# An attention kernel with a feed-forward behind it: the value products change bank and tile, the first feed-forward product its order, and the weight decoding its pace

## The chip, the cores and the metric

The kernel runs on one core of a Trainium2 chip. The metric is the time of one execution in microseconds on the device; the time before is the median of three runs. The core has TensorE (PE, matrix products, writing into the eight banks of PSUM), VectorE (DVE), ScalarE (ACT), GpSimd (POOL) and SyncE (SP), whose queue issues nearly all DMA transfers. Each engine takes its instructions in order and waits for others by semaphores.

## What is computed

Attention over 8 batches of 8 heads with 576 positions and 64 features, with a threshold below each row's maximum, and then a feed-forward layer over the 4608 tokens of 512 features:

```python
scores = scale * np.matmul(q, k.transpose(0, 1, 3, 2))
thresh = np.max(scores, axis=-1, keepdims=True) - tau
scores = np.where(scores >= thresh, scores, -1000000000.0)
attn = np.exp(scores - np.max(scores, axis=-1, keepdims=True))
attn = attn / (np.sum(attn, axis=-1, keepdims=True) + 1e-09)
attn_out = np.matmul(attn, v)
# x: the heads side by side, (4608, 512)
h = x @ w_in                       # (512, 2048)
sp = np.where(h > 20.0, h, np.log1p(np.exp(np.minimum(h, 20.0))))
return (h * np.tanh(sp)) @ w_out   # (2048, 512)
```

The weights arrive as 64-bit floats, and the kernel makes 32-bit numbers of them itself ("decoding"): one bit pattern from the upper word by a scale, a clamp, a shift and a sign, one from the lower word, and their sum; then an upper part that TensorE reads at its fast 32-bit format (hi) and a remainder (lo). Products are made from such pairs of parts.

## The kernel before

**Tiles.** Two heads make a pair; 32 pairs of 9 tiles of 128 query rows are 288 tiles, numbered g, with t = g % 9 the place in the pair. One iteration of the main loop issues the steps of several tiles, each a few tiles behind the one before: the scores of tile g+1 (`begin`; tile `s`, two buffers of two PSUM banks), the maximum, the exponential and the mask of tile g (`row_max`, `exponential`, `masked`; tiles `st`, `e`, `p`), the normalisation of g-1 on POOL, the transposes of g-2 (`transposes`; bank `tp`, and for odd tiles and t = 8 also the last keys, bank `t5`, which the profile names `t`), and the copies of g-3 out of PSUM on ACT (`evacuate`; tiles `hi`, `lo` for even and odd tiles from `tp`, `tk` from `t5`). `tp` and `t5` have one buffer each. All engines but SP are wrapped so that they keep the order in which the program issues (line 95 is that wrapper, which is why all rows of the profile carry it).

**Product with the values.** A pair's nine tiles are gathered in two groups (0 to 3 and 4 to 8). The product `y` of a group (`values_full`) is closed at t = 3 and t = 8 by `CLOSE`, `lag` = 4 tiles later, so at t = 7 and t = 3. It is cut in five chunks, which `pieces` hands out: two in an iteration before tile `SOON` = 38, five from there on. `gather` copies y on ACT into `x`; from `SOON` on in the same iteration as the last chunk, before that in the next. `y` takes one of the two buffers `ph` in the pool `psh`, which the first feed-forward product `h` takes too. When a pair is closed, `split_x` makes the parts `xh` (ACT) and `xl` (POOL) of its two token halves, two tiles apart.

**First feed-forward product.** `gemm1(b)` runs one batch behind the attention, from tile 36b + 42 on. It is a generator of 384 matmuls; `EVEN[g % 9]` says how many of them an iteration issues, none where `y` is made. For each token half c and each of the 16 feature blocks f it sums 12 matmuls into a bank `h`, which ACT copies to `hst`, and SP stores. Batches 0 to 6 take c outermost; the last one takes the feature halves outermost.

**Weights of the first product.** 32 pieces of 128 x 256 are decoded during the first tiles. `W1_STEPS` lists at which of each 18 tiles a piece is started (12 of 18). After its load, a piece goes through stages in successive iterations: two empty ones, the scaling on ACT, `clamp` (POOL), then `shift` and `sign` (DVE) and `add` (POOL), an empty one, `upper` (ACT) and `lower` (POOL, or DVE for the nine pieces of `ONV`). The sign is issued ahead of the mask of its tile before tile `JOIN` = 39, and behind it from there on.

**Queues.** SP issues the loads of q, k, v and weights and the stores of hst; a load waits there until its buffer is free, and what stands behind it in the queue waits too. Splits of q and k follow their loads two tiles later (`LOADS`).

After the attention the last batch's first product and the second product run (`w2`, `z`, `g`, `o`); the change does not touch them.

Of the kernel before, what the change touches and what calls it, by code (L numbers as in the profile page):

```python
# [15 lines left out]
B, H, S, D = 8, 8, 576, 64  # L16
NP = H // 2
LOADS = ((1, 0, 1, 3, 2, 3, 7, 3, 5, 8), (0, 3, 3, 2, 5, 4, 5, 8, 8, 9), (0, 0, 2, 4, 5, 4, 7, 6, 7, 8), (0, 0, 1, 3, 2, 3, 7, 5, 7, 8))
W1_STEPS = (1, 3, 4, 6, 7, 8, 10, 12, 13, 15, 16, 17)
STAGES = ((0, 1, 1), (0, 1, 1))  # L20
THIRD = ((),)
LAG = 2
# [7 lines left out]
SOON = 9 * FULL + 2  # L30
ONP = 1
ONV = (3, 9, 11, 12, 14, 15, 17, 18, 22)
JOIN = 39
PLAIN = (0, 1)
DM, DF = 512, 2048
ND, NF = DM // P, DF // P
# [33 lines left out]
LAST = {1: 0, 4: 1, 6: 2, 8: 3}  # L70
TURN = [[(t % 2, t // 2 * P + t % 2 * P)] for t in range(8)] + [QCOL[4]]
CLOSE = {3: 0, 8: 1}
EVEN = (14, 14, 14, 0, 13, 14, 14, 0, 13)
WIDTH = (256, 320, 320, 256)
XOFF = (0, 256, 256, 0)
SCALE = 1.0 / float(D) ** 0.5
# [42 lines left out]
class Decode:  # L119
# [16 lines left out]
        nc.scalar.activation(c, low, AF.Copy, scale=2.0**-29)  # L136

    def clamp(self):
        self.nc.gpsimd.tensor_scalar(fv(self.b), fv(self.a), TOP_MAX, -TOP_MAX, ALU.min, ALU.max)

    def shift(self):
        self.nc.vector.tensor_scalar(self.a, self.b, 3, 0x7FFFFFF8, ALU.logical_shift_left, ALU.bitwise_and)
# [18 lines left out]
def attention_moe(tc, q, k, v, tau, w_in, w_out, out):  # L161
# [3 lines left out]
    with ExitStack() as outer:  # L165
# [105 lines left out]
        with ExitStack() as first:  # L271
# [6 lines left out]
            with ExitStack() as att:  # L278
# [160 lines left out]
                def transposes(g):  # L439

                    both = tiles[g]["both"]
                    at = odd(g) * (S + D)
                    tp = pst.tile([P, 4, P], F32, name="tp")
                    for c in range(4):
                        nc.tensor.transpose(tp[:, c, :], both[:, at + c * P:at + (c + 1) * P], ident)
                    t5 = None
                    last = g < 9 * VP and g % 9 == 8
                    if odd(g) or last:
                        t5 = pst.tile([P, P], F32, name="t5")
                        if last:  # L450
                            nc.tensor.transpose(t5, both[:, S - P:S], ident)
                            nc.tensor.transpose(t5[:D], both[:, S - D:S], ident)
                        else:
                            nc.tensor.transpose(t5, both[:, 4 * P:5 * P], ident)
                    return tp, t5

                def evacuate(t, tp, t5, pt):
                    r = t // 4 if t < 8 else 1
                    if r not in pt:
                        pt[r] = [  # L460
                            ptp.tile([P, w, 320], F32, name=n, tag=n) for n, w in (("hi", 4), ("lo", 4), ("tk", 1))
                        ]
                    tail = pt[r][2][:, 0]
                    if t < 8:
                        a, at = t % 2, t // 2 % 2 * P
                        nc.scalar.copy(pt[r][a][:, :, at:at + P], tp)
                        if a:
                            nc.scalar.copy(tail[:, at:at + P], t5)
                        return
                    for a in range(2):  # L470
                        rows = slice(a * D, (a + 1) * D)
                        nc.scalar.copy(pt[r][a][:, :, 2 * P:], tp[:, :, rows])
                        nc.scalar.copy(tail[rows, 2 * P:], t5[rows, rows])
# [30 lines left out]
                    for hi, lo, t5 in tails(g):  # L504
                        nc.vector.tensor_tensor(lo, t5, fv(hi), ALU.subtract)

                def values_full(r, pt, vf, x):
                    main, tail = pt[r][:2], pt.pop(r)[2]
                    n = (2 + r) * P - r * D
                    y = psh.tile([P, 512], F32, name="y", tag="ph")  # L510

                    def chunk(c):
                        for a in range(2):
                            rows = slice(a * D, (a + 1) * D)
                            m = main[a][:, c, :n] if c < 4 else tail[:, 0, :n]
                            nc.tensor.matmul(y[rows, :n], vf[:, a, c], m, start=c == 0, stop=c == 4)

                    def gather():
                        nc.scalar.copy(x[:, r * QT:r * QT + n], y[:, :n])

                    return [lambda c=c: chunk(c) for c in range(5)], gather
# [21 lines left out]

                    return gather

                def split_x(g, x):
                    parts = []
                    for c in range(2):
                        xh = xpool.tile([P, HB], F32R, name="xh", bufs=12)
                        xl = xpool.tile([P, HB], F32R, name="xl", bufs=12)  # L550
                        parts.append((xh, xl))

                    def half(c):
                        xh, xl = parts[c]
                        sl = slice(c * HB, (c + 1) * HB)
                        nc.scalar.copy(xh, x[:, sl])
                        nc.gpsimd.tensor_tensor(xl, x[:, sl], fv(xh), ALU.subtract)

                    chores.setdefault(g + XSPLIT[1], []).append(lambda: half(0))
                    chores.setdefault(g + XSPLIT[1] + XSPLIT[2], []).append(lambda: half(1))  # L560
                    return parts
# [14 lines left out]
                def gemm1(b, xs, bank=shared, first=1):  # L576

                    halves = (range(NF // 2), range(NF // 2, NF))
                    if b < B - 1:
                        order = [(c, f) for c in range(2) for fs in halves for f in fs]
                    else:
                        order = [(c, f) for fs in halves for c in range(2) for f in fs]
                    banks = {}
                    made = {}

                    def parts(c, f, ds):
                        if (c, f) not in banks:  # L590
                            banks[c, f] = bank("h")
                        h = banks[c, f]
                        half, at = divmod(f * P, DF // 2)
                        for d in ds:
                            xh, xl = xs[d][c]
                            wh, wl = (w[:, d, at:at + P] for w in w1[half])
                            for i, (a, m) in enumerate(((wh, xh), (wh, xl), (wl, xh))):
                                nc.tensor.matmul(
                                    h[:, :HB], a, m, start=d == 0 and i == 0, stop=d == ND - 1 and i == 2
                                )  # L600
                                yield

                    def leave(c, f):
                        if f % 4 == 0:
                            made["hst"] = hp.tile([P, 4, HB], F32, name="hst", tag="hst")
                        hst, h = made["hst"], banks.pop((c, f))
                        if b < B - 1 or f % 2:
                            nc.scalar.copy(hst[:, f % 4], h[:, :HB])
                        else:
                            nc.vector.tensor_copy(hst[:, f % 4], h[:, :HB])  # L610
                        if f % 4 == 3:
                            store(nc.sync, hst, (2 * b + c) * HB, f - 3)

                    for c, f in order[:first]:
                        yield from parts(c, f, range(ND - 1))
                    for n, (c, f) in enumerate(order):
                        steps = parts(c, f, range(ND - 1, ND) if n < first else range(ND))
                        for i in range(3 if n < first else 3 * ND):
                            next(steps)
                            if i == (2 if n < first else 3 * ND - 1):  # L620
                                leave(c, f)
                            yield
# [27 lines left out]
                    made = pairs[pi]["ops"]  # L650
                    tiles[g] = dict(s=scores(t, 0 if odd(g) else D, **made))

                def product(g):
                    pi, t = divmod(g, 9)
                    pr = pairs[pi]
                    if t == (3 if pi < VP else 1):
                        pr["x"] = sm.tile([P, S], F32, name="x", bufs=2)
                    if pi < VP:
                        if t in CLOSE:
                            some, gather = values_full(CLOSE[t], pr["pt"], pr["ops"]["vf"], pr["x"])  # L660
                            pieces.extend((work, None) for work in some[:-1])
                            pieces.append((some[-1], (gather, pi if t == 8 else None)))
                    elif t in LAST:
# [1 line left out]

                def close_pair(g, pi):
                    b, hp = divmod(pi, NP)
                    batches.setdefault(b, []).append(split_x(g, pairs.pop(pi)["x"]))

                warm = psh.tile([P, P], F32, name="warm", tag="ph")  # L670

# [11 lines left out]
                    split()  # L683
                nc.vector.tensor_scalar(back, back, 1.0 / SCALE, None, ALU.mult)
                begin(0)
                for g in range(NT + 5):
                    now = [work.pop(0) for work in decoding]
                    decoding = [work for work in decoding if work]
                    if g + 1 < NT:
                        begin(g + 1)  # L690
                    ahead = 2 <= g < SOON
                    lag = 4 if g < VP * 9 + 4 or VP == NPAIRS else 5
                    if lag <= g < NT + lag and (g != VP * 9 + 4 or VP == NPAIRS):
                        product(g - lag)
                    if 3 <= g < NT + 3:
                        old = ((g - 3) % 9, *tiles[g - 3]["tp"], pairs[(g - 3) // 9]["pt"])
                        full = g - 3 < VP * 9
# [9 lines left out]
                    for _ in range(5 if g >= SOON else PIECES):  # L707
                        if pieces:
                            work, then = pieces.pop(0)
                            work()  # L710
                            if then:
                                (done if g >= SOON else ready).append(then)
                    if g < NT:
                        tiles[g]["st"], tiles[g]["e"] = row_max(tiles[g]["s"])
                    if 1 <= g <= NT:
# [257 lines left out]
```

## Time and profile before

| | |
|---|---|
| median of 3 runs | 1357.99 us (1357.27 to 1361.05) |
| the profiled execution | 1360.66 us, span 1358.9 us |
| PE busy | 1311.3 us (96%) |
| DVE, ACT, POOL busy | 872.4 (64%), 849.5 (63%), 742.3 us (55%) |
| mean granted PE clock | 0.987 |
| attention | scores of tile 0 reduced at 6.7 us, of tile 287 at 917.7 us |

Busy times are those of one execution. Rows in order of time give the start in us, the duration in us, engine, line, operation, tiles (out<-in), shapes and count, and in brackets the idle time of that engine before it and what ended it. Rows of groups give count, then busy us and mean ns of one, then idle us before them. Rows of waits give us in total, times and the longest.

### The profile page before, as it was taken

The numbers are of one execution on the slowest core, as the hardware profiler recorded it, in microseconds if no ns is written. First come the engines' busy times: TensorE is split into PE (matmuls) and PEld (weight loads), VectorE is DVE, ScalarE is ACT, GpSimd is POOL, SyncE is SP. The second block draws the span as 40 slices with busy tenths as digits, with TensorE's granted clock in tenths as the row PEclk, the third lists the DMA queues.
The fourth block names the chain that finished last, engine by engine and source line by source line (L and its number), as shares of the span: only waits on it lengthen the run. The fifth ranks groups of instructions, "written<-read, shape, count | busy, mean of one in ns | idle before, by whom it ended". The sixth has DMA issues, their size and how long they took to land. (4 is left out here: it accounts for less than half of the span.)

```text
span 1358.9 us, 28431 instructions
## 1 busy us (share of the span) xinstructions
PE 1311.3 (96%) x9941; PEld 1171.1 (86%) x9941; DVE 872.4 (64%) x2372; ACT 849.5 (63%) x1676; POOL 742.3 (55%) x1093
## 2 busy tenths in 40 slices
PE   8887999999999999999999999999999999999998
PEld 5444789988889889898888898898979999999998
DVE  6897756555556556566566556564996666666664
ACT  4777766666666666666666666665665555555552
POOL 4899966656556566566565665642403334444431
PEclk9888999999999999999999999999999999999999
DMA  6333443433333333333333333312744343444440
GB/s 175 103 92 115 150 147 89 115 95 99 107 89 97 109 103 93 98 91 114 99 94 106 89 104 102 94 53 84 253 149 155 125 137 113 141 140 137 137 131 32
DMA packets 151904, 154.83 MB, mean 114 GB/s; under 512 B 35536, under 2 KB 128720, under 8 KB 151760
## 3 DMA queue, kind: packets, MB, share of 16 engines
q1 hardware_dynamic: 151760, 153.00, 37.5%
q8 instruction: 79, 1.29, 0.4%
q14 instruction: 65, 0.53, 0.1%
HBM read 105.78 MB, written 47.19 MB: 113 GB/s over the span
## 5 line engine op out<-in xcount | busy, mean ns | idle before, releaser
L95 DVE SCALAR_TENSOR_TENSOR p<-s,st,e 128x576 f32<-128x576 f32 x288 | 235.4, 817 | 331.4 <-ACT e L95 331.0
L95 PE MATMUL h<-xh,w1h 128*128 128x288 f32 x1024 | 302.6, 295 | 1.1 <-ACT hst L95 1.1
L95 PE MATMUL h<-xl,w1h 128*128 128x288 f32 x1024 | 302.4, 295 | 0.0
L95 PE MATMUL h<-xh,w1l 128*128 128x288 f32 x1024 | 302.3, 295 | 0.0
L95 POOL TENSOR_SCALAR p<-p,st 128x576 f32<-128x576 f32 x288 | 240.3, 835 | 108.3 <-DVE st L95 89.2
L95 PE MATMUL s<-k,q 128*128 128x288 f32 (+1 forms) x1280 | 244.3, 337 | 32.4 <-DVE p L95 31.3
L95 POOL TENSOR_TENSOR z<-z 128x256 f32<-128x256 f32 x128 | 124.2, 975 | 223.1 <-DVE z L95 214.3
L95 ACT ACTIVATE e<-s,st 128x576 f32<-128x576 f32 x288 | 215.9, 750 | 45.7 <-DVE st L95 43.0
L95 PEld LDWEIGHTS s<-k,q 128*128 128x128 f32 (+1 forms) x1280 | 172.0, 192 | 55.6 <-DVE p L95 48.9
L95 DVE TENSOR_REDUCE st<-s 128x1 f32<-128x576 f32 x288 | 216.8, 753 | 2.7 <-PE s L95 2.7
L95 DVE TENSOR_TENSOR gl<-z,gh 128x1792 fp32r<-128x1792 f32 (+1 forms) x72 | 141.6, 1967 | 108.2 <-ACT gh L95 108.2
L95 ACT CAST gh<-z 128x1792 fp32r<-128x1792 f32 (+1 forms) x72 | 116.5, 1620 | 150.0 <-issue 81.2
L95 PEld LDWEIGHTS h<-xh,w1h 128*128 128x128 f32 x1024 | 192.6, 188 | 2.0 <-ACT hst L95 1.3
L95 PEld LDWEIGHTS h<-xh,w1l 128*128 128x128 f32 x1024 | 192.5, 188 | 0.0
L95 PEld LDWEIGHTS h<-xl,w1h 128*128 128x128 f32 x1024 | 192.5, 188 | 0.0
L95 PE MATMUL tp<-ident,p 128*128 128x128 f32 x1152 | 180.0, 279 | 3.9 <-POOL p L95 1.5
L95 PEld LDWEIGHTS tp<-ident,p 128*128 128x128 f32 x1152 | 135.9, 141 | 44.3 <-issue 28.6
L95 POOL TENSOR_TENSOR k<-r,k 128x320 fp32r<-128x320 f32 x112 | 97.9, 874 | 95.8 <-ACT k L95 93.6
L95 PE MATMUL y<-hi,vf 128*64 128x320 f32 (+1 forms) x512 | 145.2, 426 | 1.0 <-ACT hst L95 1.0
L95 PE MATMUL y<-lo,vf 128*64 128x320 f32 (+1 forms) x512 | 145.2, 426 | 0.0
L95 PE MATMUL o<-gh,sl 128*128 128x256 f32 x512 | 144.5, 282 | 0.0
L95 PE MATMUL o<-gl,sh 128*128 128x256 f32 x512 | 143.8, 281 | 0.0
(68 smaller groups left out, 2712.0 us busy)
## 6 DMA issues: line engine op xcount, KB each, us to landing
z<-hd SPq DMA_DIRECT2D x144, 256.0 KB, 3.1
r<-q SPq DMA_DIRECT2D x112, 160.0 KB, 2.2
r<-k SPq DMA_DIRECT2D x112, 160.0 KB, 2.4
vf<-v SPq DMA_DIRECT2D x64, 160.0 KB, 2.3
out_t<-c SPq DMA_DIRECT2D x36, 256.0 KB, 2.4
dec<-w_in SPq DMA_DIRECT2D x32, 256.0 KB, 3.2
hd<-hst SPq DMA_DIRECT2D x16, 512.0 KB, 3.3
w<-w_out SPq DMA_DIRECT2D x16, 512.0 KB, 4.5
```

Of the source, the lines that this page charges most:

```text
L95: made = method(*args, **kwargs)
```

## The change

It has five parts.

1. **Bank.** From tile `SOON` + 3 on, `y` is placed in the bank of `t5`, which grows to a whole bank for that (`own`); `psh` is left to `h`. `evacuate` copies `t5` ahead of `tp`.
2. **Tile.** The lag of the product is 5 instead of 4 from tile `SOON` + 2 on, so `y` is made at t = 8 and t = 4; `EVEN` moves its zeros there. The copy of `y` comes an iteration after its last chunk until the last tile (`NT`), not only before `SOON`. The loop has one more iteration.
3. **First batch's first product.** Batch 0 takes the feature halves outermost, and the second token half of its `xh` and `xl` lies in four more buffers of the pool `sm`.
4. **Pace.** `W1_STEPS` starts 10 pieces in 18 tiles instead of 12, so the last of the 32 is started at tile 57 instead of 48. `JOIN` = 72 puts the sign of every piece ahead of the mask.
5. **Clamp.** `clamp` goes from POOL to DVE.

```diff
-W1_STEPS = (1, 3, 4, 6, 7, 8, 10, 12, 13, 15, 16, 17)
+W1_STEPS = (1, 3, 5, 6, 8, 10, 12, 14, 15, 17)
...
-JOIN = 39
+JOIN = 72
...
-EVEN = (14, 14, 14, 0, 13, 14, 14, 0, 13)
+EVEN = (14, 14, 14, 13, 0, 14, 14, 13, 0)
...
     def clamp(self):
-        self.nc.gpsimd.tensor_scalar(fv(self.b), fv(self.a), TOP_MAX, -TOP_MAX, ALU.min, ALU.max)
+        self.nc.vector.tensor_scalar(fv(self.b), fv(self.a), TOP_MAX, -TOP_MAX, ALU.min, ALU.max)
...
-                        t5 = pst.tile([P, P], F32, name="t5")
+                        t5 = pst.tile([P, 512], F32, name="t5")[:, :P]
...
-                        nc.scalar.copy(pt[r][a][:, :, at:at + P], tp)
                         if a:
                             nc.scalar.copy(tail[:, at:at + P], t5)
+                        nc.scalar.copy(pt[r][a][:, :, at:at + P], tp)
...
-                def values_full(r, pt, vf, x):
+                def values_full(r, pt, vf, x, own):
...
-                    y = psh.tile([P, 512], F32, name="y", tag="ph")
+                    home, tag = (pst, "t5") if own else (psh, "ph")
+                    y = home.tile([P, 512], F32, name="y", tag=tag)
...
-                def split_x(g, x):
+                def split_x(g, x, early):
...
-                        xh = xpool.tile([P, HB], F32R, name="xh", bufs=12)
-                        xl = xpool.tile([P, HB], F32R, name="xl", bufs=12)
+                        home, n = (sm, 4) if early and c else (xpool, 12)
+                        xh = home.tile([P, HB], F32R, name="xh", bufs=n)
+                        xl = home.tile([P, HB], F32R, name="xl", bufs=n)
...
-                    if b < B - 1:
+                    if 0 < b < B - 1:
                         order = [(c, f) for c in range(2) for fs in halves for f in fs]
...
-                for g in range(NT + 5):
+                for g in range(NT + 6):
...
-                    lag = 4 if g < VP * 9 + 4 or VP == NPAIRS else 5
-                    if lag <= g < NT + lag and (g != VP * 9 + 4 or VP == NPAIRS):
-                        product(g - lag)
+                    lag = 4 if g < SOON + 2 else 5
+                    if lag <= g < NT + lag and g != SOON + 2:
+                        product(g - lag, g > SOON + 2)
...
-                                (done if g >= SOON else ready).append(then)
+                                (done if g >= NT else ready).append(then)
```

More of the change, by code (lines that the diff above doesn't have):

```diff
@@ L651, in begin, with product @@
                     tiles[g] = dict(s=scores(t, 0 if odd(g) else D, **made))
-                def product(g):
+                def product(g, own):
                     pi, t = divmod(g, 9)
@@ L659, in product @@
                         if t in CLOSE:
-                            some, gather = values_full(CLOSE[t], pr["pt"], pr["ops"]["vf"], pr["x"])
+                            some, gather = values_full(CLOSE[t], pr["pt"], pr["ops"]["vf"], pr["x"], own)
                             pieces.extend((work, None) for work in some[:-1])
@@ L667, in close_pair @@
                     b, hp = divmod(pi, NP)
-                    batches.setdefault(b, []).append(split_x(g, pairs.pop(pi)["x"]))
+                    batches.setdefault(b, []).append(split_x(g, pairs.pop(pi)["x"], b == 0))
                 warm = psh.tile([P, P], F32, name="warm", tag="ph")
```

## The prediction

> **What bounds the kernel now.** I read the page first, then the busy times by stage, then the waits of PE (TensorE) by stage, and last the order of time around the waits that were left. Tile n of the attention begins, in this text, where the VectorE (DVE) maximum of its scores starts.
>
> ```profile
> span 1358.9 us, 28431 instructions
> ```
> The next rows are busy times in stretches: its ends, its length, then us (and number) of PE, PE's weight loads, DVE, ACT (ScalarE) and POOL (GpSimd), and the granted clock.
> ```profile
> 110.10:132.00 21.90, 14.62 (x77) 9.21 (x77) 16.13 (x54) 14.90 (x39) 19.32 (x32) 0.83 0.31 91
> 132.00:205.40 73.40, 70.23 (x510) 60.93 (x510) 50.38 (x167) 50.65 (x126) 58.50 (x92) 0.96 0.47 145
> 205.40:917.70 712.30, 704.05 (x5419) 629.37 (x5419) 420.05 (x1569) 473.45 (x1113) 432.92 (x690) 1.00 0.34 97
> ```
> PE is full but for the beginning: from 205.4 us on it lacks 8.25 of 712.3 us. Up to tile 42, at 132 us, the first product does not exist yet; DVE and POOL are the busy ones, and just before it the granted clock is 0.83. Between 132 and 205.4 PE lacks 3.2 us, and a clock of 0.96 takes up to another 2.9. So the change can win in three places only: the time until tile 42, the 6.1 us behind it, and the 8.25 us of the long stage. The next fence has PE's largest wait in each of the stretches 6.7 to 132, 132 to 205.4 and 205.4 to 917.7 us, and one of the rest of the run (us, times, longest).
>
> ```profile
> PE s L95 <- DVE p L95: 20.2, 22, 2.1
> ...
> PE s L95 <- DVE p L95: 2.9, 4, 2.0
> ...
> PE s L95 <- DVE p L95: 8.2, 24, 0.4
> ...
> PE y L95 <- ACT hst L95: 1.0, 1, 1.0
> ```
> The 24 waits of the long stage come once in each pair of heads (9 tiles), always behind the product with the values, y. In order of time at one of them:
> ```profile
> 332.83 0.43 ACT L95 COPY x<-y 128x320 f32<-128x320 f32 x1 [2.11 <-PE y L95]
> ...
> 334.84 0.76 ACT L95 ACTIVATE e<-s,st 128x576 f32<-128x576 f32 x1
> ...
> 335.64 0.82 DVE L95 SCALAR_TENSOR_TENSOR p<-s,st,e 128x576 f32<-128x576 f32 x1 [3.01 <-ACT e L95]
> ...
> 336.52 0.80 PE L95 MATMUL s<-k,q 128*128 128x288 f32 x4 [0.35 <-DVE p L95]
> ```
> ACT stands 2.11 us at the copy of y, because the copy is issued in the tile that also issues y's matmuls. The exponential e behind it is late, DVE waits 3.01 us for e, the score bank comes free late, and PE stands 0.35 us.
>
> **The change, term by term.** The sum is made against the profiled execution: 1360.7 us, span 1358.9; the median of the runs is 1358.0, 2.7 lower, so I carry the difference over to the median.
>
> *A. Up to tile 42.* The smallest period of a tile, seen where no weight is decoded, is 2.55 us; DVE then has 0.68 us free, waiting for e:
> ```profile
> 20.07 0.82 DVE L95 SCALAR_TENSOR_TENSOR p<-s,st,e 128x576 f32<-128x576 f32 x1 [0.68 <-ACT e L95]
> ...
> 20.82 0.75 DVE L95 TENSOR_REDUCE st<-s 128x1 f32<-128x576 f32 x1
> ...
> 23.37 0.75 DVE L95 TENSOR_REDUCE st<-s 128x1 f32<-128x576 f32 x1
> ...
> 131.97 0.75 DVE L95 TENSOR_REDUCE st<-s 128x1 f32<-128x576 f32 x1
> ```
> Tile 5 starts at 20.82 and tile 42 at 131.97: 37 tiles in 111.15 us, where 37 x 2.55 would be 94.4. The excess is 16.8 us. What it is made of:
> ```profile
> L95 DVE SCALAR_TENSOR_TENSOR dec<-dec 128x256 uint32<-128x256 uint32 x24 | 13.2, 551 | 0.7
> ...
> L95 DVE TENSOR_SCALAR dec<-dec 128x256 uint32<-128x256 uint32 x24 | 12.1, 505 | 2.3 <-POOL dec L95 2.3
> ...
> L95 POOL TENSOR_SCALAR dec<-dec 128x256 f32<-128x256 f32 x24 | 9.5, 398 | 0.0
> ```
> ```profile
> L95 DVE TENSOR_SCALAR dec<-dec x32: 271/320/2421, 24.4 to 172.2; 128x256 uint32<-128x256 uint32 x32
> L95 DVE SCALAR_TENSOR_TENSOR dec<-dec x32: 411/426/1046, 24.7 to 176.3; 128x256 uint32<-128x256 uint32 x32
> ```
> The first fence has decode rows of 16.5 to 132 us, the second the same two of the whole run (min/median/max ns). The shift and the sign of a weight piece take 0.27 and 0.41 us undisturbed, together just the 0.68 that is free. They took 12.1 and 13.2 us for 24 pieces: 24 x 0.27 + 24 x 0.41 = 16.3, so 9.0 us are stretching while POOL works. Another 2.3 us DVE waited for POOL's clamp. The copy of y at tile 40 costs the rest that can be named:
> ```profile
> 124.28 0.16 DVE L95 RECIPROCAL st<-st 128x1 f32<-128x1 f32 x1
> ...
> 125.60 0.42 ACT L95 COPY x<-y 128x320 f32<-128x320 f32 x1 [4.39 <-PE y L95]
> ...
> 126.00 0.78 PE L95 MATMUL s<-k,q 128*128 128x288 f32 x4
> ...
> 127.61 0.76 ACT L95 ACTIVATE e<-s,st 128x576 f32<-128x576 f32 x1
> ...
> 129.48 0.75 DVE L95 TENSOR_REDUCE st<-s 128x1 f32<-128x576 f32 x1
> ```
> With the copy a tile later, e of tile 40 could start near 124.4 instead of 127.61. The next scores are done at 126.8 and become the late thing, so the reduction of 129.48 comes about 2.7 us earlier. After the change 20 pieces instead of 24 are shifted before tile 42 (10 instead of 12 in 18 tiles, five tiles behind their issue); 20 x 0.375 (9.0 / 24) = 7.5 us of stretching. POOL loses a clamp of 0.398 us in two of three tiles, a tenth of its time, so I take 6.8. DVE gains the clamp, which the trace has only on POOL; its nearest row is the shift, the same size and engine: 0.27 undisturbed, 0.505 as a mean, 2.42 at worst. A clamp falls in the tile before its own shift, into the free 0.68; in two tiles of 18 it meets another piece's shift: four such tiles before 42, 4 x 0.5 = 2 us. The wait for POOL's clamp goes. Of the 16.8 us, 9.0 + 2.3 + 2.7 = 14.0 become 8.8: **-5.2 us**. Ends: -14 if all of it goes; +5 if all 20 clamps are exposed at 0.505 against the 5.2.
>
> *B. 132 to 205 us.* The 2.0 us wait of the table above comes from one shift that lasted through three POOL operations:
> ```profile
> 164.95 0.82 POOL L95 TENSOR_TENSOR xl<-x,xh 128x288 fp32r<-128x288 f32 x1
> ...
> 165.03 2.42 DVE L95 TENSOR_SCALAR dec<-dec 128x256 uint32<-128x256 uint32 x1 [0.88 <-POOL dec L95]
> ...
> 165.73 0.87 POOL L95 TENSOR_TENSOR k<-r,k 128x320 fp32r<-128x320 f32 x1
> ...
> 166.55 0.73 POOL L95 TENSOR_TENSOR w1l<-dec,w1h 128x256 fp32r<-128x256 f32 x1
> ```
> The clamps are off POOL, the signs come ahead of the mask, and PE-bound tiles leave DVE slack; but decoding now goes on to tile 65. I take **-3.5** of the 6.1; ends -6.1 and +3 (12 clamps at the shift's 0.505, half of them exposed). The new order of the first product costs nothing: weights of its second half are wanted from tile 60 on (8 feature blocks in 9 tiles, twice), the last piece, issued at tile 57, is done by about 65, and the block that reads it starts near 67; with the old order it would have been wanted at 58. Four more tiles of SBUF hold the second token half; they add no instruction.
>
> *The queues.* The loads of values on SP wait for y, so they come a tile later, with the query loads queued behind them; these are read six tiles or more later, so nothing. Fewer weight loads per tile ease SP.
>
> *C. The long stage.* y's copy is now issued a tile after y, so ACT doesn't stand: **-8.2** if all 24 waits go. Late next can be y itself, 50 times, which now needs the copy of the last keys, tk, out of the same bank:
> ```profile
> 339.44 0.27 PE L95 MATMUL t<-ident,p 128*128 128x128 f32 x1
> ...
> 339.47 0.78 PE L95 MATMUL s<-k,q 128*128 128x288 f32 x4
> ...
> 340.09 0.29 PE L95 MATMUL h<-xh,w1h 128*128 128x288 f32 x1
> ...
> 340.12 0.27 ACT L95 COPY tk<-t 128x128 f32<-128x128 f32 x1
> ...
> 340.22 0.29 PE L95 MATMUL h<-xl,w1h 128*128 128x288 f32 x1
> ```
> t ends at 339.71; PE passes the scores and is ready at 340.09. With tk ahead of lo (the copy of tp, 0.59), ACT can copy from 339.75 to 340.02: PE waits for nothing to 0.1 us, if ACT is free. It need not be:
> ```profile
> 346.30 0.46 ACT L95 CAST k<-r 128x320 fp32r<-128x320 f32 x1
> 346.35 0.27 PE L95 MATMUL t<-ident,p 128*128 128x128 f32 x1
> ...
> 346.66 0.59 ACT L95 COPY lo<-tp 128x512 f32<-128x512 f32 x1
> ```
> Here ACT came free 0.1 us after t. I take 0.06 us x 50 = **+3**; ends 0 and +13 (a whole tk copy, 0.27, each time). In the other direction, t's next transposes need the bank back from the copy of y: ACT has lo (0.59), e (0.76) and the copy (0.43) to do, 1.8 us, while PE does scores and 14 h matmuls at 0.13 us spacing, 2.4 us; hidden. The splits of a batch's last pair move from tile 4 ahead of its product to tile 1 ahead: xl is ready about 4.2 us after the tile starts (lo 0.59, e, y copy, two 0.46 splits, then 0.87 and 0.81 on POOL), wanted after 4.8; six batches, **+0.5**, ends 0 and +3.
>
> *D. The end of attention.* y no longer waits for an h bank: -1.0 us. But the DVE work that ends the run waits for the last x split, which now comes after all of batch 6's matmuls:
> ```profile
> 935.58 0.43 ACT L95 COPY x<-y 128x320 f32<-128x320 f32 x1 [3.01 <-PE y L95]
> ...
> 939.61 0.69 DVE L95 TENSOR_SCALAR s<-w 128x1024 f32<-128x1024 f32 x1 [17.32 <-POOL xl L95]
> ```
> Today it starts 4.1 us behind y, 2.0 of them under 15 h matmuls; afterwards about 2.6 behind y with none: +0.5. Together **-0.5**, ends -1.5 and +1.
>
> Sum: -5.2 - 3.5 - 8.2 + 3 + 0.5 - 0.5 = -13.9; 1358.0 - 13.9 = **1344 us**.
>
> **The rivals.**
> *The port (R1).* DVE's clamps are stretched like the 2.42 us shift, and A and B give nothing: -8.2 + 3 = -5.2 with the rest, 1353. For it: POOL is 88% busy from 110 to 132 us. Against: most clamps fall in tiles without a shift.
> The Trainium skill, "SBUF — State Buffer", section "Who interferes with whom", speaks for R1: a DVE operation in a two-port mode and a GpSimd operation exclude each other for a whole instruction, whichever issues first. The trace agrees that the shift is held up, but 2.42 us through three POOL operations is more than one instruction's turn. By that rule at its hardest, each of 20 clamps behind one POOL operation of 0.87, A would pay 20 x (0.27 + 0.87) less 16 x 0.68 of free time, 11.9 in place of 2, and the time would be 1354.
> *A new wait in the long stage (R2).* y waits for tk or for its own bank about as long as PE stood before, so C is nil: -9, 1349. For it: ACT is 0.1 us late in the row above.
> *Everything goes (R3).* No half clock behind tile 42, the stretching gone: -14 - 6.1 - 8.2 - 1.5 = -30 at the most; half-way from the forecast, -22, 1336.
> *Slower (R4).* ACT is so late that y waits 0.6 us each time (lo and more ahead of tk): 50 x 0.6 = 30, against 16.9 won: +13, 1371. It turns at 0.34 us for each y. Against: the splits leave the tile before.
>
> **How the numbers follow.** Forecast 0.42, R1 0.17, R2 0.17, R3 0.17, R4 0.07. A measurement of this kernel tells about 0.3%, 4 us, from no change. The forecast's own range is 1339 to 1350. With R1, R2 and most of R3 it becomes 1334 to 1355, leaving out R4 and the far end of R3. Faster by over 0.3% (below 1353.9): forecast, R2, R3 and half of R1, 0.84; within: 0.10; slower: 0.06.
>
> **What would show it.** PE's waits for DVE's p in the long stage fall from 24 of 0.35 us to few; ACT's waits for y almost vanish; tile 42 starts near 127; no DVE wait for POOL's clamp. Waits of y for ACT's tk of over 0.1 us, or of h for POOL's xl each 36 tiles, would make C wrong; a mean DVE clamp over 0.7 us would make A and B wrong.

## The result

The changed kernel takes 1336.4 us (median of 4 runs, 1336.1 to 1336.8) against 1357.6 for the kernel before in the same comparison: ratio 0.984, 95% interval 0.9822 to 0.9858. That is 21.2 us faster; 13.9 were forecast. The time lies outside the forecast's own range (1339 to 1350 us) and inside the wider one that takes in the rivals (1334 to 1355); it is the time that the rival R3 had named (1336). The profiled execution took 1336.1 us with a span of 1334.3; its span is 24.6 us shorter than that of before, and not 21.2, mostly because the profiled execution of before (1360.7) lay 3.0 us above the median of this comparison.

The page of the kernel after, and its busy times by stretches: to tile 36, to 42, to 66 and to 287 (ends, length, PE, PE's weight loads, DVE, ACT, POOL, granted clock):

```profile
span 1334.3 us, 28422 instructions
...
PE 1297.9 (97%) x9941; PEld 1167.4 (87%) x9941; DVE 882.6 (66%) x2404; ACT 844.0 (63%) x1676; POOL 735.8 (55%) x1061
```
```profile
6.60:106.70 100.10, 82.12 (x514) 45.67 (x512) 89.46 (x305) 70.53 (x165) 70.01 (x109) 0.95 0.40 121
106.70:128.00 21.30, 14.57 (x77) 9.14 (x77) 17.89 (x56) 15.54 (x40) 17.32 (x26) 0.83 0.40 117
128.00:204.00 76.00, 75.85 (x579) 68.87 (x580) 63.49 (x205) 60.40 (x153) 67.48 (x100) 0.98 0.48 145
204.00:892.50 688.50, 688.50 (x5349) 620.06 (x5348) 414.52 (x1548) 461.62 (x1095) 428.69 (x681) 1.00 0.35 101
```
From tile 66 on PE lacks nothing at all: 688.50 of 688.50 us. From tile 42 to 66 it lacks 0.15 us of 76.0. What is left to win before the end of the attention lies ahead of tile 42, but for the granted clock of 0.98 between 42 and 66.

The same times of every kernel of this study, worked out from the starts of the score reductions. The last column is the mean length of nine tiles, one pair of heads, in the long stage: (start of tile 270 - start of tile 90) / 20. All are us.

| kernel | tile 42 at | 42 to 66 | 66 to 287 | behind 287 | a pair |
|---|---|---|---|---|---|
| before | 132.0 | 82.3 | 703.5 | 441.1 | 28.69 |
| after | 128.0 | 76.0 | 688.5 | 441.8 | 28.07 |
| e1 copy later | 129.8 | 80.5 | 715.6 | 441.8 | 29.15 |
| e2 y moved only | 132.4 | 79.4 | 688.7 | 442.1 | 28.07 |
| e3 y not moved | 129.5 | 79.1 | 703.4 | 441.2 | 28.69 |
| e4 clamp on POOL | 132.0 | 76.9 | 688.5 | 441.8 | 28.07 |
| e5 clamp only | 131.1 | 77.4 | 703.5 | 441.2 | 28.69 |
| e6 pace only | 130.5 | 80.1 | 703.3 | 441.1 | 28.68 |
| e7 tp first | 127.8 | 77.6 | 702.0 | 442.2 | 28.62 |
| e8 same tile | 128.7 | 75.9 | 688.7 | 441.6 | 28.07 |
| e9 splits moved | 131.4 | 78.3 | 689.2 | 441.2 | 28.09 |
| e10 lag only | 130.6 | 79.2 | 688.7 | 441.5 | 28.07 |
| e11 warm | 126.6 | 74.7 | 688.5 | 441.8 | 28.07 |
| e12 without bank | 125.9 | 77.0 | 689.2 | 441.1 | 28.09 |

Each row is one execution. The first two columns are uncertain: e10 and the kernel before are the same program up to tile 42, and they reach tile 36 at 108.3 and 110.1 us and tile 42 at 130.6 and 132.0. From tile 0 to 36 the granted clock was 0.95 in e10 and 0.90 before. Tile 0 itself starts at 6.3 to 7.7 us in the kernels of the table. So differences of up to about 1.8 us in the first column say nothing, and the second, in which the clock varies too, is to be read with the same care. The long stage repeats to 0.2 us.

Of the 24.6 us of the spans, 15.0 were won between tiles 66 and 287, 6.3 between 42 and 66, 4.0 ahead of 42 (2.6 if e10 stands for the kernel before); 0.7 were lost behind 287.

### The profile page after: what moved, and what is told of

The parts are those of the page before. It is cut to its first block, busy times and chain, and to the rows that moved or that the text cites. A ratio compares the mean times of both kernels' runs of the same rounds, so it can differ in the third digit from the quotient of the medians.

```text
span 1334.3 us, 28422 instructions
## 1 busy us (share of the span) xinstructions
PE 1297.9 (97%) x9941; PEld 1167.4 (87%) x9941; DVE 882.6 (66%) x2404; ACT 844.0 (63%) x1676; POOL 735.8 (55%) x1061
## 5 line engine op out<-in xcount | busy, mean ns | idle before, releaser
L95 PE MATMUL s<-k,q 128*128 128x288 f32 (+1 forms) x1280 | 241.1, 333 | 21.1 <-DVE p L95 20.0
L95 ACT ACTIVATE e<-s,st 128x576 f32<-128x576 f32 x288 | 216.1, 750 | 26.9 <-DVE st L95 23.8
L95 ACT COPY hi<-tp 128x512 f32<-128x512 f32 (+1 forms) x160 | 87.0, 544 | 169.4 <-PE tp L95 169.1
L95 PE MATMUL o<-gh,sh 128*128 128x256 f32 x512 | 143.5, 280 | 0.0
```

Source lines behind the costliest of these rows:

```text
L95: made = method(*args, **kwargs)
```

## The long stage: what the stall was, and what took it away

The stall was larger than the row that the prediction used. Waits of the long stage before the change, by PE's weight loads, which run ahead of the matmuls, and by the matmuls:

```profile
PEld s L95 <- DVE p L95: 13.9, 24, 0.6
...
PE s L95 <- DVE p L95: 8.2, 24, 0.4
PEld y L95 <- issue: 8.2, 50, 0.2
```
In order of time, at the wait that the prediction shows:
```profile
335.57 0.60 PE L95 MATMUL tp<-ident,p 128*128 128x128 f32 x4
...
336.52 0.56 PEld L95 LDWEIGHTS s<-k,q 128*128 128x128 f32 x4 [0.59 <-DVE p L95]
```
From the first start of the transposes to the start of the scores it took 0.95 us, where the others of the same shape take 0.36: 0.59 us, the number of the weight loads. The matmul's row counts only from the modelled end of the matmul before it. 24 x 0.59 = 14.2 of the 15.0 us.

After the change, in the long stage:
```profile
ACT hi L95 <- PE tp L95: 155.5, 123, 2.6
...
ACT tk L95 <- PE t L95: 37.6, 73, 1.3
...
PEld y L95 <- ACT tk L95: 8.0, 49, 0.2
```
The wait for DVE's p is gone from PE. ACT now waits for the transposes instead of y. The only wait of y is that of its weight loads for tk, 8.0 us in 49; before, the same loads stood 8.2 us in 50 with nothing to wait for, and where y follows one tile's scores it starts 0.70 us behind their start both before and after. So y's new wait costs nothing. The forecast had +3 us for it.

### Four runs that sort the parts of the move

**e2**: the changed kernel with pace, order, sign and clamp as before (parts 3 to 5 undone).

> The changed kernel with the pace, the order of the first batch's product, the place of the sign and the clamp as before; only bank, lag and copy of y are changed. Theory T: 0.62 us per pair x 27 = -17, tile 40 about -1: 1339 to 1342 us. Rival (the parts need each other, the clamp and the pace made room on VectorE and GpSimd for the long stage): no more than -8: above 1349 us.

Measured: 1343.2 us, ratio 0.9875 (0.9856 to 0.9895), a little above the range expected; a pair 28.07. The whole gain of the long stage is in parts 1 and 2, without help from the decoding.

**e1**: the kernel before and one line.
```diff
-                                (done if g >= SOON else ready).append(then)
+                                (done if g >= NT else ready).append(then)
```


> The kernel before, with one edit: ScalarE's copy of y is issued a tile after y's matmuls in the long stage too; y keeps its bank among the two of h and its lag of 4. Theory T (what counted is that ScalarE no longer stands at y's copy, but that needs a bank of y's own): the stall of 0.6 us per pair of heads goes, and y keeps one of h's two banks a tile longer. From the counts of matmuls, h wants that bank 0.6 + 3 x 0.13 = 1.0 us into the tile behind the longer y, and the copy frees it after about 1.9: a wait of 0.9 us per pair. Net +0.3 us x 25: 1357 to 1366 us. Rival (the later copy is all of it, the bank does nothing): -0.6 x 25 = -15: 1342 to 1345 us.

Measured: 1369.5 us, ratio 1.0077 (1.006 to 1.0094): slower, a pair 29.15. The wait came where the counts had put it:
```profile
PEld h L95 <- ACT x L95: 23.0, 23, 1.0
...
PE h L95 <- ACT x L95: 17.6, 23, 0.8
```
The stall of 0.6 went, and one of 1.0 us for h's bank came, once in a pair; the net 0.46 us a pair is more than the 0.3 expected, and the time lies above the range. So at this place a later copy does need a bank of its own. That is not yet the proof that the later copy was needed.

**e8**: the changed kernel with that one line put back.
```diff
-                                (done if g >= NT else ready).append(then)
+                                (done if g >= SOON else ready).append(then)
```


> The changed kernel with y's copy issued in the tile of y's last chunk again; own bank and lag 5 stay. Theory T (ScalarE standing at that copy makes the stall): the period of a pair returns from 28.07 to about 28.7 us, 15 us in all, ratio to before 0.993 to 0.996. Rival (the bank of its own and the shifted tile do the most): 0.982 to 0.988.

Measured: 1336.6 us, ratio 0.9843 (0.9827 to 0.9859): nothing is lost that could be told, and the long stage takes 688.7 us as against 688.5. ACT stands at y's copy as it did before the change, and PE does not care:
```profile
ACT x L95 <- PE y L95: 81.7, 47, 2.0
```
Here my theory fell, the one of the prediction too: that ACT stands at the copy was not what stopped PE. Left over were the bank and the tile. What else the tile decides is what stands behind the copy in ACT's queue. At t = 3 of the kernel before:
```profile
333.15 0.46 ACT L95 CAST q<-r 128x320 fp32r<-128x320 f32 x1
...
333.52 0.46 ACT L95 CAST k<-r 128x320 fp32r<-128x320 f32 x1
...
333.88 0.43 ACT L95 CAST xh<-x 128x288 fp32r<-128x288 f32 x1
...
334.21 0.58 ACT L95 COPY lo<-tp 128x512 f32<-128x512 f32 x1
...
334.69 0.27 ACT L95 COPY tk<-t 128x128 f32<-128x128 f32 x1
```
Two splits of another pair's query and key, xh, lo and tk lie between y's copy (332.83) and the exponential (334.84). At t = 4 no split of a query or key is due, and the tile behind it copies no tk.

**e9**: the kernel before, and two numbers of `LOADS`, so that the two splits come at t = 4.
```diff
-... (0, 0, 1, 3, 2, 3, 7, 5, 7, 8))
+... (0, 0, 1, 4, 2, 4, 7, 5, 7, 8))
```


> The kernel before with two numbers changed: of each later pair, one query and one key part are loaded, and so split, at t = 4 instead of t = 3, the tile in which the longer y is made and copied. The run with the copy of y back in its own tile kept the gain, so the first theory has fallen. Theory Q (the stall comes from what stands between y's copy and the next exponential on ScalarE: two splits of 0.46, xh and the transposes' copies, 2.0 us in all; without the two splits it is 0.9 shorter, more than the stall of 0.6): the period of a pair falls from 28.69 to about 28.1 us, ratio 0.988 to 0.992, with y's bank, lag and copy as before. Rival (a copy of y out of a bank shared with h must cost a stall wherever it stands): 0.998 to 1.002.

Measured: 1341.7 us, ratio 0.9874 (0.9859 to 0.9889), a pair 28.09. With y's bank, lag and copy untouched, two numbers give the gain of e2. (The loads and the POOL halves of the two splits move with them; the chain of waits, from the copy over e and p to the scores, runs through ACT.) The same tile of e9:
```profile
325.89 0.43 ACT L95 COPY x<-y 128x320 f32<-128x320 f32 x1 [2.11 <-PE y L95]
...
327.33 0.76 ACT L95 ACTIVATE e<-s,st 128x576 f32<-128x576 f32 x1
...
328.12 0.82 DVE L95 SCALAR_TENSOR_TENSOR p<-s,st,e 128x576 f32<-128x576 f32 x1 [2.43 <-ACT e L95]
...
329.00 0.79 PE L95 MATMUL s<-k,q 128*128 128x288 f32 x4
```
ACT waits the same 2.11 us for y, but e follows the copy's start by 1.44 us instead of 2.01, DVE's wait for e shrinks from 3.01 to 2.43, and PE's scores wait for nothing. The 0.57 us that came out is just the 0.59 of the stall; I had expected 0.9. The scores still start 0.06 us behind the end of p, as before, so there is nothing to spare.

**e10**: the kernel before with the lag of 5 and the zeros of `EVEN` a tile later; shared bank, copy in the same tile.

> The kernel before with the lag of 5 and the moved zeros alone: y is made a tile later, in the shared bank of h, and copied in the same tile. Theory Q: at t = 4 and t = 8 no split stands behind y's copy but xh, so the period is about 28.1 us and the ratio 0.987 to 0.991: the bank of its own buys nothing. Rival (the bank buys half or more of it): 0.994 or more.

Measured: 1342.7 us, ratio 0.988 (0.9866 to 0.9895), a pair 28.07. The bank of its own and the later copy add nothing that can be measured here. Behind y's copy stand only xh and hi here, so the tk copy has left with the splits; e9 shows that moving the splits is enough.

**e7**: the changed kernel with `tp` copied ahead of `t5` again.

> The changed kernel with tp copied ahead of t5, as before the change. tk then ends 0.68 us behind the end of t instead of 0.31, and y's first matmul stands at 0.46. Theory T (y really waits for its bank, and the order of the two copies is what makes that free): 0.28 us x 50 = +14 on the changed kernel, 0.6 us per pair more, ratio to before 0.993 to 0.996. Rival (PE has other slack): the changed kernel's ratio, 0.982 to 0.986.

Measured: 1351.8 us, ratio 0.9948 (0.9931 to 0.9966), a pair 28.62. The longer wait, first of y's weight loads and then of its matmuls:
```profile
PEld y L95 <- ACT tk L95: 20.2, 46, 0.4
...
PE y L95 <- ACT tk L95: 9.5, 46, 0.2
```
0.28 us for each y, from start to start, as reckoned (0.98 us from the scores' start to y instead of 0.70). Once y sits in that bank, the order of the two copies is worth what the whole move wins.

## The decoding

Decode rows of the kernel after, from 16.5 to 132 us, to be held against the 24 pieces before:
```profile
L95 DVE SCALAR_TENSOR_TENSOR dec<-dec 128x256 uint32<-128x256 uint32 x21 | 12.4, 590 | 0.6
L95 DVE TENSOR_SCALAR dec<-dec 128x256 f32<-128x256 f32 x22 | 9.9, 451 | 0.0
...
L95 DVE TENSOR_SCALAR dec<-dec 128x256 uint32<-128x256 uint32 x21 | 6.9, 328 | 0.0
```
The clamp (second row) takes 0.451 us on DVE, 0.18 over its 0.27; the shift behind it takes 0.328 instead of 0.505, the sign 0.590 instead of 0.551. Stretching is 3.9 + 1.2 + 3.8 = 8.9 us, as much as the 9.0 before with more pieces. What went is the wait for POOL's clamp (2.3 us), and DVE's waits for e fell from 12.7 to 8.9 us in that window: the clamp lies in time that DVE had waited. Moving the clamp alone shows the same: 15.2 us in e4 against the 8.9, and 8.6 in e5 against the 12.7. Not in this sum are the eight remainders `w1l` that DVE makes in the window: 6.2 us instead of 4.7.

**e4**: the changed kernel with `clamp` on `nc.gpsimd`.

> The changed kernel with the clamp back on GpSimd. Theory of the prediction (the clamp on GpSimd makes VectorE wait, 4.8 us in all before, and loads GpSimd): 1338 to 1341 us. Rival (on VectorE it is stretched by GpSimd and costs as much as it saves): 1335 to 1337 us.

Measured: 1340.4 us, ratio 0.9859 (0.9843 to 0.9875), tile 42 at 132.0. This is in the range of the prediction's theory, but the intervals of e4 and of the changed kernel overlap, so e4 alone doesn't settle the clamp's worth. Tile 42 comes 4.0 us later than in the changed kernel, of which up to 1.8 can be the spread of single executions.

**e5**: the kernel before with `clamp` on `nc.vector`.

> The kernel before with the clamp on VectorE, nothing else. In the run with the clamp put back on GpSimd, tile 42 started at 132.0 us as before the change, and at 128.0 with it on VectorE. Theory T (the clamp alone makes the faster start, the pace has no part in it): tile 42 at 128 to 129 us, time 4 to 6 us under before (ratio 0.9955 to 0.997). Rival (with 12 pieces in 18 tiles VectorE has no room for it; it pays only at the slower pace): tile 42 at 131 us or later, ratio 0.998 or more.

Measured: 1355.0 us, ratio 0.9967 (0.9954 to 0.998), as expected in the time but not in the place: tile 42 at 131.1, where the rival had put it, and 4.9 us won between 42 and 66, where DVE no longer waits for POOL's clamp (2.5 us before). The interval is clear of no change.

**e6**: the kernel before with parts 3 and 4 (pace, order, sign).

> The kernel before with the slower pace, the new order of the first batch's product and the sign ahead of the mask; clamp on GpSimd, y as before. Theory T: tile 42 at 132 us as before, 2 to 3 us won between tiles 42 and 66: ratio 0.9975 to 0.9985. Theory of the prediction (fewer pieces, less stretching): tile 42 near 130, ratio below 0.997.

Measured: 1357.1 us, ratio 0.9988 (0.9978 to 0.9999): 1.6 us, between 0.1 and 3.0; the median gain is smaller than either theory had it. Tile 42 is at 130.5, within the spread of the kernel before.

**e3**: parts 3 to 5 together on the kernel before.

> The changed kernel with bank, lag and copy of y as before; pace, order, place of the sign and clamp are changed. Theory T (the parts add up): what e2 doesn't give of the 21, 3 to 5 us: 1352 to 1355 us. Rival (decoding gave the larger share): below 1349 us.

Measured: 1352.5 us, ratio 0.995 (0.9935 to 0.9965), 6.8 us. With the 17.0 of e2 that is 23.8 against 21.8 for all of it (0.984 of 1360.8): within the intervals, 2 to 3 us to either side, the parts add up.

## What was left in front: the clock

In the changed kernel tile 40 still takes 6.4 us (6.2 before). y's last matmuls before the first product run from 117.3 to 121.8 us, and the granted clock is half from 114.0 to 120.8:
```profile
114.00:120.80 6.80, 5.49 (x22) 3.00 (x22) 6.28 (x22) 3.97 (x9) 6.44 (x10) 0.50 0.19 48
```
```profile
121.83 0.66 PE L95 MATMUL tp<-ident,p 128*128 128x128 f32 x4
...
122.64 0.27 ACT L95 COPY tk<-t 128x128 f32<-128x128 f32 x1 [3.98 <-PE t L95]
...
123.28 0.76 ACT L95 ACTIVATE e<-s,st 128x576 f32<-128x576 f32 x1
```
The wait of ACT for y (4.39 us before) has become one for the transposes that PE makes behind y, and e stands behind that copy. The 2.7 us that the prediction counted here were turned into a new wait.

**e11**: the changed kernel, and
```diff
+                    elif 28 <= g < 42:
+                        warm_up(6)
```


> The changed kernel with six transposes of the identity more in each of the tiles 28 to 41, whose result nobody reads. In the changed kernel the granted clock is 0.50 from 114.0 to 120.8 us, in the last y before the first product, and ScalarE then stands 4.0 us at the transposed keys. Theory W (a busier TensorE keeps its clock, and y takes 2.8 instead of 4.4 us): tile 42 starts 1.5 to 3 us earlier than 128.0, 0.1 to 0.2% under the changed kernel. Rival (the transposes stand in the way of scores, or the clock falls all the same): no gain, or up to 3 us slower.

Measured: 1333.3 us, ratio 0.9811 (0.9796 to 0.9825). In its stretches to tile 42 and to 66 the clock is whole:
```profile
106.90:126.60 19.70, 16.18 (x123) 12.49 (x119) 17.91 (x58) 15.46 (x40) 17.40 (x25) 1.00 0.40 122
126.60:201.30 74.70, 74.58 (x579) 67.61 (x580) 64.14 (x207) 60.26 (x153) 67.49 (x100) 1.00 0.48 149
```
```profile
ACT tk L95 <- PE t L95: 2.4, 1, 2.4
```
ACT's wait at tile 40 fell from 4.0 to 2.4 us. Tile 40 takes 4.8 us instead of 6.4, tile 42 starts 1.4 us earlier, and 1.3 more are won up to 66 at full clock.

**e12**: the kernel before with the two numbers of e9, parts 3 to 5 and the transposes of e11; bank, lag and copy of y as before.

> The kernel before with the two numbers of e9, the pace, the order, the sign's place and the clamp of the change, and the transposes of e11; bank, lag and copy of y stay as before. Theory Q (bank, lag and later copy are only another way around the two splits): the period is 28.1 us and the time that of e11 within 0.3%: ratio 0.979 to 0.985. Rival (the bank or the later copy is worth something beside faster decoding, in the first tiles above all, where y is copied at tile 39): 0.986 or more.

Measured: 1333.4 us, ratio 0.9804 (0.9787 to 0.982). It is as fast as e11 within what can be told; both medians lie 3 us under the changed kernel's; e12's interval is just clear of the changed kernel's, e11's just touches it. Bank, lag and later copy are one way around the two splits; the two numbers are another, for the same time.

## Why the prediction was right, step by step

The direction was right, the wide range held, and the stall named in C was the one that went. The forecast's own range didn't hold, three sizes were off, and the reason given in C was wrong. That the time is R3's is chance: R3 came to it half-way between the forecast and a sum with 14 us ahead of tile 42, the stretching gone, and 8.2 in the long stage. Measured were 4.0 us ahead of tile 42, with 8.9 us of stretching left, and 15.0 in the long stage. The terms are held here against the spans, 24.6 us apart.

- **C, the long stage: -4.7 forecast, -15.0 measured** (up to tile 287). Three things. The stall was read off the matmul's row (8.2 us) where the weight loads' row (13.9) has its full length; that is the largest error. y's wait for tk (+3) and the splits' late xl (+0.5) did not appear: no wait of h for xl stands in the long stage's list, and the wait for tk, at 8.0 us in 49 over the 0.1 us that the prediction had set as a sign against C, only took the place of one that had been there before. And the reason was wrong: "y's copy is now issued a tile after y, so ACT doesn't stand" is true and without effect on the long stage (e8). The lag took y away from the tile of the two splits (e9, e10), which the prediction did not name as part of the stall.
- **B, 132 to 205 us: -3.5 forecast, -6.3 measured.** Nearly all of the idle time and half of the clock's loss went; PE is full from tile 42. Of the parts, y's move gave 2.9 (e2) and the decoding 3.2 (e3; the clamp by itself 4.9, e5); these are single executions, and the clamp's larger number than the decoding's shows how far they can be trusted. No cost of the longer decoding is seen: with the pace alone (e6) the stretch takes 80.1 us, not more than the 82.3 before.
- **A, up to tile 42: -5.2 forecast, -4.0 measured** (-2.6 against e10), from other parts. The 2.7 us at tile 40 did not come: a wait of 4.0 us for the transposes took the place of the one for y. Shift and sign are stretched by 5.0 us instead of the 6.8 reckoned, for which the clamp is stretched by 3.9 and not 2: 8.9 in all, where 8.8 were forecast. The gain lies ahead of tile 40, and the decoding alone has it: counted from the start of tile 0, tile 40 starts at 116.6 us before (115.1 in e10), at 111.8 after and at 111.3 in e3. That e3 is only 2.5 us ahead at tile 42 comes from tile 40, which takes 8.0 us there: DVE stands at a remainder whose upper part ACT makes behind the copy of y.
```profile
DVE w1l L95 <- ACT w1h L95: 4.5, 1, 4.5
```
  With the copy a tile later that wait is gone and tile 40 takes 6.4 us; with the copy back in its tile (e8) it is there again, 3.9 us, and tile 40 takes 7.5. So at this one tile the later copy has an effect, of about 1 us, too little to be told in the whole time. What the clamp and the pace give by themselves ahead of tile 42 (0.9 and 1.5 us) is within the spread.
- **D: -0.5 forecast, +0.7 measured.** y's wait for h's bank went (1.0 us), but h now waits in that stretch, in two rows for 1.8 and 0.5 us, where it had waited 1.1:
```profile
PE h L95 <- ACT hst L95: 1.8, 2, 1.1
...
PE h L95 <- ACT x L95: 0.5, 1, 0.5
```
What of that costs the 0.7 was not tried.
- **R1** did not come true: the mean clamp on DVE takes 0.451 us, under the 0.7 that the prediction had set as the sign, and the clamp alone makes the kernel faster (e5). The rule of the Trainium skill, "SBUF — State Buffer", section "Who interferes with whom", that a two-port DVE operation and a GpSimd operation exclude each other, agrees with the trace: the clamp is stretched by 0.18 us on average, and one that began at 96.98 us, 0.05 us into a GpSimd operation of 0.74, took 0.85. By DVE's waits for e, the move paid because DVE had time to spare, 0.68 us in a tile without decoding. **R2** did not come true either: C gave 15.0 us and not nil. **R4**'s price is what e7 measured, at 0.28 us for each y instead of 0.6.

## What to carry to other kernels

When an engine stands at a copy out of PSUM, ask what is queued behind the copy and ahead of the work that the bottleneck waits for; moving two unrelated splits by one tile can be worth as much as a new bank, a longer lag and a later copy. Read a stall of TensorE from start to start: the matmul's idle time fell short of it here (0.35 for 0.59 us), the weight loads' idle time hit it there but went beyond it in e7 (0.44 for 0.28). Where two executions of one program differ by 1.8 us, don't share out smaller gains among the parts. An operation that is moved to an engine costs by where in that engine's waits it falls, and a short wait that repeats in each round is room for it.

## What was not expected of the hardware

- A DVE shift of 0.27 us took 2.42 us through three GpSimd operations in a row before the change. No DVE decode operation of the kernel after takes over 1.1 us; why that one did not get its turn between two of them stays open.
- The granted clock fell to half at 114.0 us in the kernel after although PE, by the profile, was busy for 4.27 of the 6.80 us before, with no wait of over 1.7 us by the matmuls' rows or 2.0 by the weight loads':
```profile
107.20:114.00 6.80, 4.27 (x29) 2.97 (x28) 6.76 (x23) 5.82 (x17) 6.26 (x9) 1.00 0.40 128
```
  Six dummy transposes in each of the tiles 28 to 41 kept it whole: its mean is 0.996 to 0.999 in the five executions of e11, 0.992 to 0.993 in the four of the changed kernel. The Trainium skill, "TensorE: Matmul & The Clock Gate", section "What's actually happening", gives an idle window of about 3.4 us as the reason for half clock; no wait of that length stands in these 6.80 us, so too small a share of work in a window fits it better than an idle one. No run here measures that share.
- One program can lose the clock at different times: between 6.5 and 57 us it was 0.93 in the kernel before and 1.00 in e10, between 57 and 80 us 0.85 and 1.00, and between 80 and 110 us 0.89 and 0.83, with the same instructions. The two are 1.8 us apart at tile 36.
